# A two-part attention kernel: its output projection on four column tiles, with eight rows a segment projected later

## The chip, the cores and the metric

The kernel runs on one core of one Trainium2 chip. The metric is the device time of one execution in microseconds. A core has five engines that run side by side and wait for each other by semaphores: PE (matrix multiplication), DVE and ACT (vector and scalar work; they copy results out of PSUM), POOL, and SP, which here only issues transfers. Sixteen DMA engines carry the transfers.

## The reference

Part A is a local attention over 2048 rows (32 heads of 20, a window of 8 rows, two apart). The change does not touch it. Part B is an attention with a recurrent memory: 64 segments of 32 rows, each behind 8 memory rows that are the previous segment's output.

```python
M, seg = 8, 32                      # Dm = 640, H = 32 heads of Dh = 192, L = M + seg = 40
mem = mem0
for s in range(64):
    h = concatenate([mem, x[:, 32 * s:32 * s + 32]], axis=1)       # 40 rows
    q, k, v = h @ Wq, h @ Wk, h @ Wv                               # 640 -> 32 x 192 each
    p = softmax(where(mask, q @ k.T * scale, -1e9))                # a row sees the memory and rows up to its own
    o = (p @ v) @ Wo                                               # 32 x 192 -> 640
    mem = o[:, :M]                                                 # the next segment's memory
    outs.append(o[:, M:])
```

The first 8 of the 40 output rows are needed at once, for the next segment. The other 32 are only output.

## The kernel before, in words

Part A comes first. Part B is then a loop of 64 calls of `segment(s)`, and nearly the whole time is spent there. The order of the PE instructions is the order of the program text (a manual schedule); the other engines' instructions are placed by a scheduler.

*Rows.* The 40 rows of a segment are kept as 32 "main" rows (8 memory rows and the first 24 rows of x) and 8 "late" rows (the last 8 of x). A pass over the main rows is `project32` (line 443): 32 rows fill 32 columns of the array, so four matmuls with 384 columns of the weights each run on four column tiles at once. The late rows of four segments are projected together, 32 at a time, ahead of their use, which is what `ahead`, `turn_late` and the tables `STREAMED` and `RENEW` are about; each segment renews one k group and one v group in this way, and the q group of the next segment.

*Groups.* The 32 heads are worked on in four groups of 8. For each group: `project_qk` (q and k, turned by `turn` so that heads lie on partitions), `scores` (line 515), `softmax`, `put_p`, `turn_p` (line 547), `values`, `mix` (line 564; the copies of its four results into the tile `OT` are line 423's, on ACT and DVE in turn), and `project_out(Y, g)` (line 578). OT holds, for each of the group's 12 chunks of 128 rows of (head, element), 40 columns: 32 main rows and 8 late rows. The groups are interleaved by hand in `segment`, so that PE has other work while a softmax or a copy is under way.

*Output projection.* The 24 weight units `o` hold two chunks each. For each chunk two matmuls of 64 columns of OT (40 rows and 24 columns that are not used) and 320 columns of the weights run on two column tiles, one for each half of the 640 outputs, and all 48 chunks are summed in the PSUM tile `Y`. At the end of the segment one ACT copy moves Y into `row` (line 643), `memory_rows` (line 589) turns the first 8 rows and puts them into the next segment's input `HX`, and two transfers on POOL's queue write 32 rows of output (line 650). The last matmuls of the look-ahead q projection stand between project_out(Y, 3) and memory_rows.

*Weights.* Some of the weight units stay in SBUF, and 23 of them do not: 13 of q, k and v with 384 KB and 10 of `o` with 320 KB. They are copied once into DRAM (`wcopy_...`) and loaded again in every segment, through a ring of five slots named `t`: `get_unit` (line 394) issues the load on SP's queue, in the order of use. The load into a slot waits until the matmuls of the unit that used it five places before have ended. SP's queue also loads the next segment's rows, once a segment.

The functions that the change touches:

## Time and profile before

| | |
|---|---|
| median of 3 runs | 2027.26 us (2017.42 to 2029.16) |
| the profiled execution | 2024.66 us, of it 2022.8 us span |
| PE busy | 1945.4 us, 96% of the span |
| DVE, ACT, POOL busy | 1128.3, 725.6, 193.6 us |
| queue of SP's transfers | 87.9% of the 16 DMA engines' time |
| all transfers | 596.29 MB, 295 GB/s in the mean |
| granted PE clock | 0.994 of full speed |

The profile is of one execution. Its groups of instructions give the busy time, the number and the mean length of each kind, and the idle time ahead of them with what ended it; its chain of waits follows the work that ended last, back from the end, each step to what released it. Matmuls are pipelined: several are under way at once, and a matmul's length is not its share of PE's time; that is read from how far apart blocks of them start. A segment takes 28 to 29 us.

### The profile page before, as it was taken

To read this page: it belongs to the slowest core of one execution; us is meant where nothing else is said; L and a number is where in the kernel's file an instruction comes from. 1 tells how busy PE (TensorE), PEld (TensorE's weight loads), DVE (VectorE), ACT (ScalarE), POOL (GpSimd) and SP (SyncE) were. 2 spreads that over 40 slices of the span, in tenths; PEclk is the share of its full clock that TensorE was granted. 3 is DMA by queue.
4 is the path that set the end of the run, shared out by engine and by line. 5 is a ranking of instruction groups with operands and counts; after the bars stand their busy time and mean duration, and the time that the engine had idled before them with its cause. 6 is when DMAs were issued, how large, how long until landed. Compare 5 with 4: busy or idle time off the path is not lost.

```text
span 2022.8 us, 97144 instructions
## 1 busy us (share of the span) xinstructions
PE 1945.4 (96%) x42512; PEld 1243.6 (61%) x42512; DVE 1128.3 (56%) x3622; ACT 725.6 (36%) x2126; POOL 193.6 (10%) x674
## 2 busy tenths in 40 slices
PE   7989999999999999999999999999999999999998
PEld 4656666666666666666666666666666665666665
DVE  5875555555555455555555555555555554555554
ACT  3543333333333333333333333333333333333333
POOL 2000000110001101001001001101001001110110
PEclk9999999999999999999999999999999999999999
DMA  9927999999899999999999989999899988989997
GB/s 343 311 76 269 311 300 305 301 302 307 290 305 304 299 288 312 302 304 303 303 299 297 308 292 311 305 303 299 296 298 303 298 304 284 303 293 300 305 302 257
DMA packets 270123, 596.29 MB, mean 295 GB/s; under 512 B 61065, under 2 KB 72841, under 8 KB 269385
## 3 DMA queue, kind: packets, MB, share of 16 engines
q1 hardware_dynamic: 264770, 585.97, 87.9%
q8 instruction: 333, 5.46, 1.1%
q0 software_dynamic: 4928, 4.11, 0.6%
q14 instruction: 92, 0.75, 0.1%
HBM read 576.85 MB, written 18.87 MB: 295 GB/s over the span
## 4 chain that ended last, share of the span: by engine, by line
PE 71%; DMA 19%; DVE 6%; ACT 1%; issue 1%; SPq 1%; POOL 0%; DVEq 0%; POOLq 0%; ACTq 0%
PE acc L443 33%; PE Y L578 18%; DMA t<-wcopy_k 8%; DMA t<-wcopy_o 6%; PE pt L456 6%; PE Sps L515 4%; PE OTps L564 4%; PE pq L95 2%; PE pt L547 2%; DVE sb L423 2%; DMA out_dram<-row 2%; DMA t<-wcopy_v 1%; PE po L161 1%; DMA wcopy_o<-in_B_Wo_dram 1%; PE py L172 1%
## 5 line engine op out<-in xcount | busy, mean ns | idle before, releaser
L443 PEld LDWEIGHTS <-HX 128*32 128x32 bf16 x19380 | 462.7, 96 | 274.3 <-issue 46.5
L578 PEld LDWEIGHTS <-OT 128*64 128x64 bf16 x6144 | 316.8, 109 | 131.0 <-ACT OT L423 20.0
L578 PE MATMUL Y<-wres_o,OT 128*64 128x320 bf16 x3584 | 344.3, 302 | 2.2
L443 PE MATMUL acc<-wres_q,HX 128*32 128x384 bf16 x6460 | 332.6, 328 | 0.5 <-ACT sb L423 0.2
L443 PE MATMUL acc<-t,HX 128*32 128x384 bf16 x4200 | 309.1, 328 | 12.9 <-DMA t<-wcopy_k 10.1
L578 PE MATMUL Y<-t,OT 128*64 128x320 bf16 x2560 | 277.7, 303 | 10.0 <-DMA t<-wcopy_o 9.2
L423 DVE CAST sb<-acc 128x384 bf16<-128x384 f32 x322 | 178.8, 556 | 186.6 <-PE acc L443 171.3
L443 PE MATMUL acc<-wres_v,HX 128*32 128x384 bf16 x4844 | 276.5, 328 | 0.1
L528 ACT ACTIVATE t<-t 128x160 f32<-128x160 f32 x256 | 86.1, 336 | 439.4 <-DVE t L527 439.4
L443 PE MATMUL acc<-wres_k,HX 128*32 128x384 bf16 x3876 | 224.8, 327 | 0.3 <-issue 0.3
L522 DVE SCALAR_TENSOR_TENSOR t<-Sps,mask 128x160 f32<-128x160 f32 x256 | 82.8, 323 | 214.6 <-PE Sps L515 186.6
L423 ACT CAST sb<-acc 128x384 bf16<-128x384 f32 x324 | 153.6, 474 | 125.1 <-PE acc L443 123.5
L456 PE MATMUL pt<-ident,sb 128*128 128x128 bf16 x1938 | 179.4, 221 | 6.9 <-DVE sb L423 1.7
L423 DVE CAST OT<-OTps 128x120 bf16<-128x120 f32 x512 | 125.5, 271 | 97.4 <-PE OTps L564 96.8
L488 POOL COPY QT<-Lb 128x96 bf16<-128x96 bf16 x252 | 67.4, 267 | 1112.0 <-PE Sps L515 955.2
L456 PEld LDWEIGHTS <-sb 128*128 128x128 bf16 x1938 | 110.2, 97 | 82.3 <-issue 32.3
L515 PEld LDWEIGHTS <-QT 128*64 128x64 bf16 (+1 forms) x4096 | 118.9, 109 | 55.1 <-issue 40.5
L423 ACT CAST OT<-OTps 128x120 bf16<-128x120 f32 x512 | 106.0, 258 | 110.7 <-PE OTps L564 110.4
L515 PE MATMUL Sps<-KT,QT 128*64 128x40 bf16 (+1 forms) x4096 | 137.0, 188 | 2.2 <-DVE KT L423 1.0
L530 DVE TENSOR_REDUCE sm<-t 128x4 f32<-128x160 f32 x256 | 81.8, 320 | 78.7 <-ACT t L528 78.7
L564 PEld LDWEIGHTS <-Vst 32*128 32x128 bf16 (+1 forms) x4096 | 62.2, 97 | 82.3 <-issue 60.5
L564 PE MATMUL OTps<-PT,Vst 32*128 32x40 bf16 (+1 forms) x4096 | 109.7, 192 | 0.0
(75 smaller groups left out, 1916.0 us busy)
## 6 DMA issues: line engine op xcount, KB each, us to landing
t<-wcopy_o SPq DMA_DIRECT2D x640, 320.0 KB, 4.3
t<-wcopy_k SPq DMA_DIRECT2D x512, 384.0 KB, 4.8
t<-wcopy_v SPq DMA_DIRECT2D x320, 384.0 KB, 4.8
wres_q<-in_B_Wq_dram SPq DMA_DIRECT2D x20, 384.0 KB, 7.7
wres_v<-in_B_Wv_dram SPq DMA_DIRECT2D x15, 384.0 KB, 7.8
wres_k<-in_B_Wk_dram SPq DMA_DIRECT2D x12, 384.0 KB, 7.7
wres_o<-in_B_Wo_dram SPq DMA_DIRECT2D x14, 320.0 KB, 6.7
wcopy_o<-in_B_Wo_dram SPq DMA_DIRECT2D x10, 320.0 KB, 8.1
```

The source lines that it names most:

```text
L95: nc.tensor.matmul(pq[32 * d:32 * d + 32], lhsT=wcol[:, k, t, 4 * c + d, :], rhs=xTs[s][:, k, :], start=(k == 0), stop=(k == 4), tile_posi ...
L423: (nc.scalar.copy if copies["n"] % 2 else nc.vector.tensor_copy)(dst, src)
L443: nc.tensor.matmul(ps[n][32 * j:32 * j + 32, :], lhsT=X[:, dc, :], rhs=w[:, 384 * j:384 * j + 384], start=(dc == 0), stop=(dc == 4), tile_ ...
L456: nc.tensor.matmul(pt[:, c], lhsT=sb[:, 128 * c:128 * c + 128], rhs=ident, start=True, stop=True)
L488: nc.gpsimd.tensor_copy(tokens(T)[:, :, 32:L], b[:])
L515: nc.tensor.matmul(Sps[64 * g2:64 * g2 + 64, a, :], lhsT=QT[lo:hi, L * cc:L * cc + 64], rhs=KTt[lo:hi, cc, :], start=(g2 not in seen), sto ...
L522: nc.vector.scalar_tensor_tensor(out=t1[:], in0=Sps[:], scalar=scale, in1=mask[:].unsqueeze(1).to_broadcast([128, 4, L]), op0=ALU.mult, op ...
L528: nc.scalar.activation(t1[:], t1[:], ACTF.Exp)
L530: nc.vector.tensor_reduce(out=sm[:], in_=t1[:], axis=AX.X, op=ALU.add)
L547: nc.tensor.transpose(pt[:, late, :], P[:, late].rearrange("p a n -> p (a n)"), ident)
L564: nc.tensor.matmul(dst, lhsT=V[32 * a:32 * a + 32, e0:e1], rhs=PT[32 * a:32 * a + 32, late, half, :], start=(wide and late == 0 and half = ...
L578: nc.tensor.matmul(Y[64 * gv:64 * gv + 64, :], lhsT=OT[:, L * c:L * c + 64], rhs=w[:, n:n + 320], start=(i == 0 and r == 0), stop=(i == 23 ...
```

## The change

- `project_out` takes the 32 main rows alone. The two chunks of a unit go to four column tiles of 32: even chunks to rows 0 to 63 of Y (a half of the outputs in each 32), odd chunks to rows 64 to 127. `add_pairs` adds the two, with two ACT copies and two DVE additions, into a buffer of the tag `Vst`.
- The 8 late rows of OT are copied on POOL into a tile `OL` after each `mix`; once a segment OL goes to a DRAM tile `OW`. In the last segment they are loaded back, 16 segments at a time, into the places of resident weights that are no longer used (`joined` makes one tile of those), and `project_late` projects 128 rows at a time behind the last segment, with the whole array.
- Of the five weight chunks of the look-ahead q projection, one instead of three stands before project_out(Y, 3), and four instead of two behind it.
- The tables of streamed units change: 12 of k and v and 11 of `o` are streamed in a segment, 23 as before.

```diff
-STREAMED = {"k": ((0, 4), (0, 4), (0, 3), (0, 3)), "v": ((0, 1), (1,), (2,), (2,)),
-            "o": (0, 4, 6, 8, 11, 14, 17, 18, 22, 23)}
+STREAMED = {"k": ((0, 3), (0, 2, 4), (0, 3), (3,)), "v": ((0, 3), (1,), (1,), ()),
+            "o": (0, 4, 5, 6, 9, 11, 12, 16, 18, 22, 23)}
 SLOT = 1536
 RENEW = {0: ("k0", "v2"), 1: ("k1", "v3"), 2: ("k2", "v0"), 3: ("k3", "v1")}
 BLOCKS = 18
...
         v = t[:, 0:unit_cols(u)]
         return v.rearrange("p (k d) -> p k d", k=2) if u[0] == "o" else v
+    joined = {("q", 0): [], ("q", 1): [], ("q", 2): [], ("v", 1): []}
+
     def place_resident(pool, units):
         for u in units:
-            res[u] = pool.tile([128, unit_cols(u)], BF16, name="wres_%s%d_%d" % u)[:]
+            part = joined.get(u[:2])
+            if part is None:
+                res[u] = pool.tile([128, unit_cols(u)], BF16, name="wres_%s%d_%d" % u)[:]
+                continue
+            if not part:
+                n = sum(v[:2] == u[:2] for v in units)
+                part.append(pool.tile([128, n, 1536], BF16, name="wres_%s%d" % u[:2]))
+            res[u] = part[0][:, sum(v[:2] == u[:2] for v in res), :]
     def load_resident(units, engs):
         for k, u in enumerate(units):
...
     place_resident(respool, resident[:n_pre])
     dpool = ctx.enter_context(tc.tile_pool(name="b_copy", bufs=1, space=bass.MemoryType.DRAM))
     XW = dpool.tile([n_seg, 2 * SEG, Dm], BF16, name="xwindows")
+    OW = dpool.tile([n_seg, 128, 48 * M], BF16, name="olate")
     def copy_windows():
...
     P = cpool.tile([128, 2, 4, 32], BF16, name="P")
-    OT = cpool.tile([128, 12 * L + PADW], BF16, name="OT")
+    OT = cpool.tile([128, 12 * L], BF16, name="OT")
+    OL = cpool.tile([128, M, 48], BF16, name="OL")
     free = [cpool.tile([128, 12, M], BF16, name=f"Lb{i}") for i in range(BLOCKS)]
     late = {}
     LV = [cpool.tile([128, 384], BF16, name=f"Lv{g}") for g in range(GROUPS)]
     nc.gpsimd.memset(P[:], 0.0)
-    for t in [QT, OT]:
-        nc.gpsimd.memset(t[:, t.shape[1] - PADW:], 0.0)
+    nc.gpsimd.memset(QT[:, 12 * L:], 0.0)
     copies = {"n": 0}
...
                                          tile_position=(32 * a, col))
         for a in range(4):
             evacuate(OT[:, 3 * L * a:3 * L * a + 3 * L], ps[a][:].rearrange("p k n -> p (k n)"))
+        nc.gpsimd.tensor_copy(OL[:, :, 12 * g:12 * g + 12].rearrange("p n c -> p c n"), tokens(OT)[:, :, 32:L])
     def project_out(Y, g, pairs=range(6)):
         for a in pairs:
...
             for r in range(2):
                 c = 2 * a + r
                 for gv in range(2):
-                    n = 640 * r + 320 * gv
-                    nc.tensor.matmul(Y[64 * gv:64 * gv + 64, :], lhsT=OT[:, L * c:L * c + 64],
-                                     rhs=w[:, n:n + 320], start=(i == 0 and r == 0), stop=(i == 23 and r == 1),
-                                     tile_position=(0, 64 * gv))
+                    n, at = 640 * r + 320 * gv, 64 * r + 32 * gv
+                    nc.tensor.matmul(Y[at:at + 32, :], lhsT=OT[:, L * c:L * c + 32], rhs=w[:, n:n + 320],
+                                     start=(i == 0), stop=(i == 23), tile_position=(0, at))
+
+    def add_pairs(Y):
+        t1 = one.tile([128, 4, L], FP32, tag="t1")
+        odd = t1[:].rearrange("p a n -> p (a n)")
+        Ysb = one.tile([128, 384], BF16, tag="Vst")
+        for h in range(2):
+            nc.scalar.copy(odd[64 * h:64 * h + 64, :], Y[64:128, 160 * h:160 * h + 160])
+        for h in range(2):
+            nc.vector.tensor_tensor(out=Ysb[0:64, 160 * h:160 * h + 160], in0=Y[0:64, 160 * h:160 * h + 160],
+                                    in1=odd[64 * h:64 * h + 64, :], op=ALU.add)
+        return Ysb
     def memory_rows(s, Ysb):
         pt = ps_x.tile([128, 5, M], FP32, tag="x")
...
                 c0, c1 = max(128 * dc, 320 * gv), min(128 * dc + 128, 320 * gv + 320)
                 if c0 < c1:
                     lo = c0 - 128 * dc
-                    nc.tensor.matmul(pt[lo:lo + c1 - c0, dc, :], lhsT=Ysb[:, c0 - 320 * gv:c1 - 320 * gv],
-                                     rhs=ident[:, 64 * gv:64 * gv + M], start=True, stop=True,
+                    nc.tensor.matmul(pt[lo:lo + c1 - c0, dc, :], lhsT=Ysb[0:64, c0 - 320 * gv:c1 - 320 * gv],
+                                     rhs=ident[0:64, 32 * gv:32 * gv + M], start=True, stop=True,
                                      tile_position=(0, lo))
         nc.vector.tensor_copy(HXs[(s + 1) % 2][:, :, 0:M], pt[:])
+
+    LATE = n_seg // 4
+
+    def late_tokens(b):
+        wide = joined[(("q", 0), ("q", 1), ("q", 2), ("v", 1))[b]][0]
+        return wide[:].rearrange("p n c -> p (n c)")[:, 0:LATE * 48 * M]
+
+    def load_late(b):
+        nc.gpsimd.dma_start(late_tokens(b).rearrange("p (s n) -> p s n", s=LATE), OW[LATE * b:LATE * b + LATE].rearrange("s p n -> p s n"))
+
+    def project_late(b):
+        X = late_tokens(b).rearrange("p (t c) -> p t c", c=48)
+        ps = [ps_acc.tile([128, 384], FP32, tag="acc", name=f"late{gv}") for gv in range(2)]
+        for i in range(24):
+            w = get_unit(("o", i, 0))
+            for r in range(2):
+                c = 2 * i + r
+                for gv in range(2):
+                    n = 640 * r + 320 * gv
+                    nc.tensor.matmul(ps[gv][:, 0:320], lhsT=X[:, :, c], rhs=w[:, n:n + 320],
+                                     start=(c == 0), stop=(c == 47))
+        rows = out2.rearrange("(s n) d -> s n d", n=SEG)[LATE * b:LATE * b + LATE, SEG - M:SEG]
+        for gv in range(2):
+            if gv:
+                y = one.tile([128, 384], BF16, tag="Vst", name="y")[:, 0:320]
+            else:
+                y = one.tile([128, 4, L], FP32, tag="t1", name="y")[:].rearrange("p a n -> p (a n)").bitcast(BF16)
+            evacuate(y, ps[gv][:, 0:320])
+            nc.gpsimd.dma_start(rows[:, :, Dm + 320 * gv:Dm + 320 * gv + 320], y)
     def segment(s):
         last = s + 1 == n_seg
...
         project_out(Y, 1, range(4, 6))
         mix(2, PT[2], V[2])
         V[3] = values(s, 3)
+        if last:
+            load_late(0)
+            load_late(1)
+            load_late(2)
         project_out(Y, 2, range(0, 4))
         PT[3] = turn_p()
         project_out(Y, 2, range(4, 6))
         mix(3, PT[3], V[3])
+        nc.gpsimd.dma_start(OW[s], OL[:].rearrange("p n c -> p (n c)"))
+        if last:
+            load_late(3)
+        else:
+            gl = (s + 1) % 4
+            ql = project32([ahead(s + 1)], "q", gl, range(0, 1))
+        project_out(Y, 3)
+        Ysb = add_pairs(Y)
         if not last:
-            gl = (s + 1) % 4
-            ql = project32([ahead(s + 1)], "q", gl, range(0, 3))
-        project_out(Y, 3)
-        row = one.tile([128, 4, L], FP32, tag="t1")
-        Ysb = row[:].rearrange("p a n -> p (a n)").bitcast(BF16)
-        nc.scalar.copy(Ysb, Y[:])
-        if not last:
-            project32([ahead(s + 1)], "q", gl, range(3, 5), ql)
+            project32([ahead(s + 1)], "q", gl, range(1, 5), ql)
             sb = to_sb(ql[0])
             memory_rows(s, Ysb)
             turn_late(sb, "q", gl, s, s + 1)
         for gv in range(2):
-            nc.gpsimd.dma_start(out2[SEG * s:SEG * s + SEG, Dm + 320 * gv:Dm + 320 * gv + 320],
-                                Ysb[64 * gv + M:64 * gv + L, :])
+            nc.gpsimd.dma_start(out2[SEG * s:SEG * s + SEG - M, Dm + 320 * gv:Dm + 320 * gv + 320],
+                                Ysb[32 * gv + M:32 * gv + 32, 0:320])
     load_x(0)
     load_resident(early, [nc.sync])
     with tc.manual_schedule(engines={mybir.EngineType.PE}):
         for s in range(n_seg):
             segment(s)
+        for b in range(4):
+            project_late(b)
 def run_all(ctx, tc, A_x, A_wqkv, A_wo, B_x, B_mem0, B_Wq, B_Wk, B_Wv, B_Wo, out, ident):
```

## The prediction

> **What bounds the kernel now.** I read the head of the page first, then the chain of waits in one segment of part B, then the groups of instructions, and last the transfers. The page:

> ```profile
> PE 1945.4 (96%) x42512; PEld 1243.6 (61%) x42512; DVE 1128.3 (56%) x3622; ACT 725.6 (36%) x2126; POOL 193.6 (10%) x674
> q1 hardware_dynamic: 264770, 585.97, 87.9%
> t<-wcopy_o SPq DMA_DIRECT2D x640, 320.0 KB, 4.3
> t<-wcopy_k SPq DMA_DIRECT2D x512, 384.0 KB, 4.8
> ```

> PE is busy 96% of the span, but the 16 DMA engines are busy 88% as well, nearly all with weights that part B streams anew in every segment: 23 units through five slots `t`. A unit takes 4.3 us (320 KB) or 4.8 us (384 KB) from issue to landing. Who waits, on PE:

> ```profile
> PE acc L443 <- DMA t<-wcopy_k: 10.1, 32, 0.9
> PE Y L578 <- DMA t<-wcopy_o: 9.2, 23, 0.8
> PE pt L547 <- DVE P L540: 6.1, 23, 0.7
> ```

> So PE sets the pace, and waits for units only 10.1 + 9.2 us, with 1.1 us for v: 0.3 us in each of 64 segments. The chain shows one stretch of a segment and how near the transfers are (start, length, what):

> ```profile
> 1024.44 0.93 PE acc L443 x20
> 1025.36 0.39 PE OTps L564 x32
> 1025.76 0.93 PE acc L443 x20
> 1026.68 0.27 PE pt L456 x3
> ...
> 1026.96 0.33 PE pt L547 x2
> 1027.29 1.79 PE Y L578 x24
> ...
> 1030.57 4.79 DMA t<-wcopy_o
> 1035.36 0.04 issue
> 1035.40 0.46 PE Y L578 x4
> ...
> 1036.26 1.74 PE acc L443 x40
> 1038.00 1.21 PE Y L578 x16
> ...
> 1041.08 1.75 PE Y L578 x24
> ```

> Forty matmuls of line 443 take 1.74 us and twenty 0.93 us, so one of 384 columns on four column tiles costs 0.81 / 20 = 40.5 ns. Twenty-four of project_out (line 578, 320 columns on two column tiles) take 1.75 us and sixteen 1.21 us: 67.5 ns each. The chain runs through a 4.79 us transfer although PE hardly idles: ring and PE are both nearly critical. The span is 2022.8 us, the profiled execution 2024.66 us; sums are made against the latter, 2.6 us below the median of the runs (2027.26).

> **What the change removes.** project_out goes from two tiles of 64 columns to four of 32, with the same 96 matmuls a segment. The nearest row is line 443, the same shape with 384 columns: 40.5 x 320/384 = 33.8 ns. Each saves 33.7 ns, 96 x 33.7 = 3.24 us a segment, 64 segments: **-207 us**. Bounds: nothing (if line 443's rate did not carry over) and -207; I take the whole, since only the column count differs.

> **What it adds at the segment's end.** Two covers get thinner: eight matmuls of the look-ahead q projection move from before project_out(Y, 3) to after it, and one ACT copy of Y becomes add_pairs: two ACT copies, then two DVE adds. The end before (start, length):

> ```profile
> 1040.59 0.42 ACT L423 CAST OT<-OTps 128x120 bf16<-128x120 f32 x2 [0.84 <-PE OTps L564]
> 1041.01 0.46 PE L578 MATMUL Y<-t,OT 128*64 128x320 bf16 x4
> 1042.92 0.43 ACT L643 CAST row<-Y 128x320 bf16<-128x320 f32 x1 [1.90 <-issue]
> 1043.40 0.47 PE L589 MATMUL pt<-ident,row 128*128 128x8 bf16 x6
> 1044.21 1.00 PE L443 MATMUL acc<-wres_q,HX 128*32 128x384 bf16 x20
> ```

> mix(3) starts at 1040.02, so the next segment starts 4.19 us later. After: the first quarter of OT is copied 0.57 us after mix(3)'s start for 0.21 to 0.26 us, so project_out starts at about 0.88 (0.99 before). It lasts 0.81 us, and Y is readable at about 1.98. Then two ACT copies of 64x160 at about 0.29 (128x160 bf16 is 0.29 on ACT; the bounds are 0.24 for 96 columns and 0.34 for line 528's exp), and one DVE add after the last copy at 0.32 (line 522's 128x160 from PSUM). With 0.06 us between engines memory_rows starts at about 3.05. From there to the next segment's first matmul was 0.81 us: 3.86. The end gains 0.33 us where the 24 matmuls alone would give 0.81: 0.48 back, x63 = **+30 us** (15 to 45).

> **What else loses its cover.** turn_p(3) comes a median 0.71 us after its P is ready (0.50 to 1.3), and 24 faster matmuls lie between scores(3) and it, 0.81 us less: about 0.15 us of new wait. The QT and KT copies of scores(3) had 0.58 us to spare and lose 0.54; mix(3)'s PT copy had 0.31 and loses 0.27: 0.05 together. 0.2 x 64 = **+13 us** (5 to 30).

> **Off the path.** POOL gets four copies to OL a segment, at 0.27 us each by line 488's 128x96 rows, and one more issue (0.5 us by line 650): 1.6 us in 26 on an engine that is 10% busy. In its order each OL copy stands right after its mix, and the next mix's copies into OT, which wait for it, come over 2 us later. Behind it on POOL stand the late-token copies for QT and KT that scores waits for; with 1 us spare there I cost it at nothing. If that cover went, each stalled mix would cost 0.3 us, 77 us in all. The issue of OW[s] stands ahead of the two output issues and of the next QT copy, which scores(0) wants only some 6 us later. The output's tile is now a `Vst` buffer, whose next writer is values(0), later than `t1`'s.

> **The late rows.** Four batches of 24 units x 4 = 384 matmuls of the full array. The nearest row is part A's output line 172, 128x320, which starts one every 136 ns: 52 us. In the five-slot ring, 11 streamed units a batch and some pairs with 3.7 us between them (need below) give about 1.3 us a batch, 5 us; three hand-overs of a PSUM tile to its evacuation 2 us. The last copy and output issue resemble today's tail. **+59 us** (54 to 72). load_late issues 2048 short rows four times on POOL; the nearest rows are 0.50 us for 32 and 0.55 us for 128 rows, which gives 1.6 us, or 8 us by a proportion: once, **+3 us** (0 to 25), while 6.3 MB more cross the DMA engines.

> **The ring, the largest unknown.** Bytes a segment stay (8192 KB before, 8128 KB and 96 KB of OL after), as do the 23 units, but the segment gets shorter. A slot is free when its unit's last matmul ends; the unit five places on is then issued. I call lead the PE work from that last matmul's start to that fifth unit's first. It must cover the matmul's own 0.30 us (302 ns is the mean of one in the group of line 578), about 0.1 us of issue and semaphores at both ends, and the landing: 4.7 us for o, 5.2 for k and v. Before, the same adding gives no lead under 4.5 us and a handful at 4.5 to 5.0, in keeping with 0.3 us of waits. After, one at a time:
> - o5 follows the slot of k2's chunk 0: 0.74 + 0.39 + 0.93 + 0.27 + 0.33 from the chain above and 20 matmuls of project_out at 33.8 ns, 0.68: 3.3 us. In the two kinds of segment (of four) that also renew k2 or v1, 4.1. Short by 1.4 or 0.6, mean 1.0.
> - o23 follows o11: about 4.1 us, 4.9 where v3 is renewed. Mean 0.4.
> - k2's chunk 0 has 4.4 us in half of the segments: mean 0.4. v0's 4.7 in half: 0.25. o0 and o4: 0.1.
> These make 2.1 us a segment. A wait lengthens the leads that hold it, so not all add up; 1.3 to 2.1, and I take 1.6, which is 1.3 more than now: **+83 us** (20 if landings get shorter, 200 if the fuller ring lengthens them).

> Sum: -207 + 30 + 13 + 59 + 3 + 83 = -19; 2024.66 - 19 = 2006, and I say **2005 us**. Of a gain of 207 us nine tenths are spent again.

> **Rivals.**
> *The ring keeps up.* The landings above are those of a loaded queue. A 10 KB SP transfer lands in 2.3 us by the page and 384 KB at the 403 GB/s of the window from 1015 to 1020 us takes 0.98: 3.3 us on an empty queue. Against it: the queues are 88% busy and medians are 4.3 and 4.8. If needs fell to about 4 us, only o5 would wait, some 0.2 us, and the time would be 2024.66 - 207 + 30 + 13 + 55 + 3 - 8 = 1911; halfway, 1955. [...]

> *The ring takes over: slower.* PE no longer idles the queue, so four or five units are always under way, and landings go to 5.2 us for o and 5.7 for k and v (in the chain around 1012 us one took 6.11 us). Each lead short now is short by another 0.9, and o0, o4, o18 and o22 join: about 3.5 us a segment, 3.2 more than now, +205: 2127. The middle, 2.4 more: 2075. It decides from 1.6 us of added waits a segment; 0.1 us of landing is worth some 25 us. The 385 to 400 GB/s of single windows against the 300 of the mean speak against it.

> *The array doesn't run four tiles of 320 columns as it does of 384.* Then nothing is saved and 100 us are added: 2130. Line 443 speaks against it.

> **How the numbers follow.** The forecast, 1980 to 2035, 0.50; the ring keeps up 0.22; the ring takes over 0.24; four tiles gain nothing 0.04. Faster by over 1% (what a measurement of this kernel can tell; below about 2004) is the second and half of the first: 0.46. Within 1%: most of the rest of the first and a little of the third, 0.28. Slower: 0.26. The range, 1945 to 2075, leaves out the far ends of the two ring cases.

> **What would show it.** Per-segment matmul time of project_out near 3.3 us; PE waits for `t<-wcopy_o` and `t<-wcopy_k` of 60 to 130 us in all, most of them at o5 and o23; waits for add_pairs before memory_rows of about 0.5 us a segment; segments of about 27 us; 55 to 65 us behind the last segment. It is wrong if landings move by over 0.2 us either way, if OT's copies wait for POOL, or if project_out's matmuls do not halve.

## The result, and the profile after

The changed kernel takes **2138.97 us** (median of 4 runs, 2124.48 to 2144.14), the kernel before, on the same chip, 2028.21 us (4 runs, 2017.42 to 2034.18). The ratio is 1.0541, with a 95% interval of 1.0473 to 1.0609: slower by 5.4%, where 2005 us was forecast. The profiled execution took 2138.64 us, of it 2136.9 us span, 114 us more than the one before. The granted PE clock was 0.970 of full speed (0.994 before).

The page of the changed kernel (engines: busy time, share, instructions; the queue of SP's transfers: packets, MB, share of the 16 DMA engines' time; the shares of the chain; ring units: number, size, median us from issue to landing):

```profile
PE 1897.7 (89%) x42896; PEld 1156.5 (54%) x42896; DVE 1187.4 (56%) x3754; ACT 741.1 (35%) x2194; POOL 412.5 (19%) x1005
q1 hardware_dynamic: 271106, 596.20, 83.7%
PE 48%; DMA 41%; issue 5%; DVE 4%; ACT 1%; SPq 1%; POOL 0%; POOLq 0%; ACTq 0%; DVEq 0%
t<-wcopy_o SPq DMA_DIRECT2D x748, 320.0 KB, 4.5
t<-wcopy_k SPq DMA_DIRECT2D x512, 384.0 KB, 5.1
```

PE is busy for 48 us less, and the span is longer: PE waits. The chain that ended last runs through transfers for 41% of the span, where it had been 19% (and PE 71%). Landings moved by only 0.2 and 0.3 us. The waits of the changed kernel (what waited, for what: us in all, times, longest):

```profile
PE Y L589 <- DMA t<-wcopy_o: 69.7, 100, 2.5
PE acc L453 <- DMA t<-wcopy_k: 56.5, 103, 2.8
PE pt L610 <- DVE Ysb L599: 34.9, 122, 0.4
PE Y L589 <- DVE OT L433: 6.6, 30, 0.5
PE acc L453 <- DMA t<-wcopy_v: 5.5, 8, 2.2
PE Y L589 <- ACT OT L433: 4.9, 29, 0.2
```

Waits for ring units are 131.7 us against 20.4 before. New are the waits of memory_rows (line 610) for add_pairs (line 599): about two in each segment. How the chain passes through one segment (start, length, what):

```profile
1006.47 0.89 PE Y L589 x20
...
1007.79 7.16 DMA t<-wcopy_k
1014.94 0.04 issue
1014.99 0.35 PE acc L453 x4
1015.33 0.48 PE Sps L525 x16
...
1019.26 4.82 DMA t<-wcopy_o
1024.08 0.04 issue
1024.12 0.32 PE Y L589 x4
```

Twenty matmuls of project_out take 0.89 us at 1006.47, so the array does run four tiles of 320 columns as fast as hoped. But two transfers, 7.16 and 4.82 us, fill 12 of the 17 us that follow: PE has other work during most of them, but it reaches the unit before the transfer has landed, and from there the transfer sets the time. The groups (out<-in, shapes, number | busy us, mean ns | idle before, what ended most of it):

```profile
L589 PE MATMUL Y<-t,OT 128*32 128x320 bf16 x2816 | 218.9, 307 | 84.6 <-DMA t<-wcopy_o 69.7
L589 PE MATMUL Y<-wres_o,OT 128*32 128x320 bf16 x3328 | 184.7, 302 | 1.2 <-issue 1.2
...
L579 POOL COPY OL<-OT 128x96 bf16<-128x96 bf16 x256 | 173.4, 677 | 657.7 <-DVE OT L433 388.6
...
L498 POOL COPY QT<-Lb 128x96 bf16<-128x96 bf16 x252 | 67.5, 268 | 744.4 <-PE Sps L525 676.2
```

PE idles for 1.2 us ahead of the project_out matmuls with resident weights and for 84.6 us ahead of those with streamed ones. The copies to OL take 677 ns where the other 128x96 copy takes 268.

**Where the 114 us are.** I split each profiled execution into part A with segment 0, the next 62 segments (from one segment's first memory_rows matmul to the next's), and the rest. Before: 216.7, 62 x 28.60, 32.8. After: 217.4, 62 x 29.17, and 111.2, which is 42.8 for the last segment and 68.4 for the late rows and the tail. So the loop lost 35 us instead of gaining 78, and the end cost 78 us instead of 59.

### The profile page after: what moved, and what is told of

It is laid out like the page before. It is cut to its first block, busy times and chain, and to the rows that moved or that the text cites. A ratio compares the mean times of both kernels' runs of the same rounds, so it can differ in the third digit from the quotient of the medians.

```text
span 2136.9 us, 98886 instructions
## 1 busy us (share of the span) xinstructions
PE 1897.7 (89%) x42896; PEld 1156.5 (54%) x42896; DVE 1187.4 (56%) x3754; ACT 741.1 (35%) x2194; POOL 412.5 (19%) x1005
## 4 chain that ended last, share of the span: by engine, by line
PE 48%; DMA 41%; issue 5%; DVE 4%; ACT 1%; SPq 1%; POOL 0%; POOLq 0%; ACTq 0%; DVEq 0%
PE acc L453 24%; DMA t<-wcopy_o 21%; DMA t<-wcopy_k 16%; PE Y L589 7%; PE Sps L525 5%; PE pt L466 4%; PE OTps L574 2%; PE pq L95 2%; DMA t<-wcopy_v 2%; PE pt L557 1%; DMA wcopy_o<-in_B_Wo_dram 1%; PE po L161 1%; DMA xwindows<-in_B_x_dram 1%; SPq L366 1%; DVE prod L151 0%
## 5 line engine op out<-in xcount | busy, mean ns | idle before, releaser
L453 PEld LDWEIGHTS <-HX 128*32 128x32 bf16 x19380 | 490.9, 98 | 350.7 <-issue 121.7
L453 PE MATMUL acc<-t,HX 128*32 128x384 bf16 x3876 | 300.8, 336 | 63.7 <-DMA t<-wcopy_k 56.5
L453 PE MATMUL acc<-wres_q,HX 128*32 128x384 bf16 x6460 | 348.1, 339 | 1.0 <-ACT sb L433 0.3
L579 POOL COPY OL<-OT 128x96 bf16<-128x96 bf16 x256 | 173.4, 677 | 657.7 <-DVE OT L433 388.6
L453 PE MATMUL acc<-wres_v,HX 128*32 128x384 bf16 x5168 | 296.8, 334 | 1.4 <-issue 1.4
L589 PE MATMUL Y<-t,OT 128*32 128x320 bf16 x2816 | 218.9, 307 | 84.6 <-DMA t<-wcopy_o 69.7
L453 PE MATMUL acc<-wres_k,HX 128*32 128x384 bf16 x3876 | 254.3, 335 | 0.3 <-ACT sb L433 0.3
L589 PEld LDWEIGHTS <-OT 128*32 128x32 bf16 x6144 | 146.2, 96 | 187.7 <-issue 103.6
L498 POOL COPY QT<-Lb 128x96 bf16<-128x96 bf16 x252 | 67.5, 268 | 744.4 <-PE Sps L525 676.2
L589 PE MATMUL Y<-wres_o,OT 128*32 128x320 bf16 x3328 | 184.7, 302 | 1.2 <-issue 1.2
L525 PEld LDWEIGHTS <-QT 128*64 128x64 bf16 (+1 forms) x4096 | 108.7, 110 | 72.8 <-issue 51.7
## 6 DMA issues: line engine op xcount, KB each, us to landing
t<-wcopy_k SPq DMA_DIRECT2D x512, 384.0 KB, 5.1
t<-wcopy_v SPq DMA_DIRECT2D x256, 384.0 KB, 4.9
wres_q<-in_B_Wq_dram SPq DMA_DIRECT2D x20, 384.0 KB, 7.7
wres_v<-in_B_Wv_dram SPq DMA_DIRECT2D x16, 384.0 KB, 7.7
wres_k<-in_B_Wk_dram SPq DMA_DIRECT2D x12, 384.0 KB, 7.3
```

Of the source, the lines that this page charges most:

```text
L453: nc.tensor.matmul(ps[n][32 * j:32 * j + 32, :], lhsT=X[:, dc, :], rhs=w[:, 384 * j:384 * j + 384], start=(dc == 0), stop=(dc == 4), tile_ ...
L498: nc.gpsimd.tensor_copy(tokens(T)[:, :, 32:L], b[:])
L525: nc.tensor.matmul(Sps[64 * g2:64 * g2 + 64, a, :], lhsT=QT[lo:hi, L * cc:L * cc + 64], rhs=KTt[lo:hi, cc, :], start=(g2 not in seen), sto ...
L579: nc.gpsimd.tensor_copy(OL[:, :, 12 * g:12 * g + 12].rearrange("p n c -> p c n"), tokens(OT)[:, :, 32:L])
L589: nc.tensor.matmul(Y[at:at + 32, :], lhsT=OT[:, L * c:L * c + 32], rhs=w[:, n:n + 320], start=(i == 0), stop=(i == 23), tile_position=(0, at))
```

## The experiments

Times are medians; "a segment" is the mean of the 62. Unless it says otherwise an edit is one to the changed kernel.

**Without the ring, changed kernel and kernel before.** Streamed units are read from resident ones instead (o from o1, k and v from q3's chunk of the same number), so no weights are loaded in the loop and the outputs are not the reference's.

```diff
             return res[u]
+        return get_unit(("o", 1, 0) if u[0] == "o" else ("q", 3, u[2]))
         t = wstream.tile([128, SLOT], BF16, tag="ws")
```

> Leaves out: the changed kernel with every streamed weight unit replaced by one that stays in SBUF, so the five-slot ring carries nothing (wrong weights, the same matmuls). Theory 1 (ring): the changed kernel's segments lose about 2.4 us each to waits for units and its last segment and late rows some 25 us more, so this comes to 1950 to 1975 us, segments of 26.0 to 26.5 us. Theory 2 (clock): PE at half clock in 31 windows of 3.4 to 10 us is what costs; then little is won here, over 2050 us, and the granted clock falls further, because PE is denser. Theory 3 (POOL's copies to OL, 0.68 us each, hold OT): over 2050 us as well, with the clock as now.

> The same done to the kernel before: all streamed units replaced by resident ones. Theory 1: it loses only its 0.3 us of waits a segment, 2028 - 20 = about 2005 us; the gap to the changed kernel without its ring is then what the change is worth on PE alone, about -40 us (-207 for project_out, +160 for the rest). Theory 2: the two without a ring differ by less than that, or the changed one is slower, by its clock.

Measured: the changed kernel 1899.98 us, ratio 0.9369 (0.9345 to 0.9394); the kernel before 1978.66 us, 0.9757 (0.9731 to 0.9782). The page of the changed kernel without a ring:

```profile
PE 1804.4 (95%) x42896; PEld 1124.8 (59%) x42896; DVE 1183.4 (62%) x3754; ACT 737.5 (39%) x2194; POOL 413.3 (22%) x1005
q1 hardware_dynamic: 52802, 49.01, 8.4%
```

On PE alone the change is worth -79 us: segments of 25.76 against 27.83 us (-2.07), and 86.3 us behind the loop against 32.5 (+54). The granted clock is 0.996 without the ring, where theory 2 had it fall further. The ring costs the kernel before 49 us and the changed kernel **239 us**, 0.77 and 3.41 us a segment. That settles which side the loss is on. Both times lie below what the ring theory gave (1950 to 1975 and about 2005 us): the ring costs more than the waits for units that it counted. The rest asks what the 239 us are made of.

**x set to zero** (the rows of part B are copied from a DRAM tile of zeros), because the clock had fallen from 0.994 to 0.970.

> The changed kernel with part B's input rows all zero (the windows are copied from a block of zeros), every instruction and transfer as it is. [...] Theory 2: the half-clock windows of part B vanish (granted clock over 0.99) and the time falls by 30 to 45 us, to about 2100. Theory 1: the clock may recover, but PE then waits for units instead; 2120 to 2139 us.

Measured: 2143.6 us, ratio 1.058 (1.0532 to 1.0629), clock 0.968. The clock is hardly another with zeros (0.968, against 0.970 in the changed kernel), and theory 2, which expected over 0.99, is out: that the data set the clock was my assumption, and no run shows it.

**Without the late rows** (no copy to OL, no OW, no load_late, no project_late; the last 8 output rows of each segment are missing).

```diff
-        nc.gpsimd.tensor_copy(OL[:, :, 12 * g:12 * g + 12].rearrange("p n c -> p c n"), tokens(OT)[:, :, 32:L])
...
-        nc.gpsimd.dma_start(OW[s], OL[:].rearrange("p n c -> p (n c)"))
...
-        for b in range(4):
-            project_late(b)
```

> The changed kernel without the late rows: no copies to OL, no transfer of OL, nothing loaded back, no late projection (eight output rows a segment are not written). Theory 1: the segments stay at 29.2 us and only the end goes, about 78 us: 2055 to 2065 us. Theory 3: the segments get shorter as well, by 0.4 us or more each, and the time is below 2035 us.

Measured: 2051.2 us, ratio 1.013 (1.0084 to 1.0176). A segment takes 28.91 us, 0.26 less (theory 3 asked for 0.4): that is all that POOL's long copies and OL's transfers can cost in the loop. The end falls from 111.2 to 33.4 us.

**Where the next segment's rows are loaded.** In both kernels SP's waits for that load had looked suspicious: 76 us in the kernel before, 146 in the changed one, with ring loads queued behind.

```diff
-        load_x(s + 1)
         tq, tk, V, PT = {}, {}, {}, {}
...
         V[0] = values(s, 0)
+        load_x(s + 1)
```

> The changed kernel with load_x(s + 1), the load of the next segment's rows, placed behind values(s, 0) instead of at the head of the segment; it needs its buffer only at the segment's end. So far it stands in SP's queue ahead of the weight loads for the segment's first k units and waits there for PE (146 us in all, 76 before the change), while slots come free behind it. Theory 1a (the queue is held up at the segment's head): the waits at k1's chunks 2 and 4, about 1.0 us a segment, go; segments 28.0 to 28.3 us, 2060 to 2085 us. Theory 1b (the DMA engines' load alone sets the landings): the same waits turn up elsewhere, 2125 to 2145 us.

> The kernel before with the same later place of load_x. Theory 1a: its ring costs 49 us by the run without a ring, of which the units at the head of the segment hold about a third: 2005 to 2020 us. Theory 1b: 2020 to 2032 us.

Measured: 2141.11 us, 1.0549 (1.0498 to 1.0601), and for the kernel before 2027.17 us, 1.0007 (0.9987 to 1.0027). That theory fell: nothing moves.

**The old table of streamed units, and the old cover** (three chunks of the look-ahead q ahead of project_out(Y, 3)).

```diff
-            ql = project32([ahead(s + 1)], "q", gl, range(0, 1))
+            ql = project32([ahead(s + 1)], "q", gl, range(0, 3))
...
-            project32([ahead(s + 1)], "q", gl, range(1, 5), ql)
+            project32([ahead(s + 1)], "q", gl, range(3, 5), ql)
```

> The changed kernel with the table of streamed units of the kernel before (13 of k and v, 10 of o): as many units, 64 KB more a segment, other places. Theory 1c (places: a unit waits where the PE work between its slot's release and its use is short): the waits at o5 (0.8 us a segment) and k1 go, those at o23 stay, and some new ones come at the v0 pair; 2075 to 2110 us. Theory 1b: the load is the same, so 2130 to 2150 us.

> The changed kernel with the look-ahead q projection split as before the change: three chunks before project_out(Y, 3) and two behind it. My price for the new split was 0.2 us a segment at OT's copies against 0.32 at add_pairs. The lead of o23 grows by 0.3 us here and the wait for add_pairs by 0.3: 2130 to 2145 us, no change. If the end of the segment were what costs, it would move by over 20 us.

Measured: the old table 2113.93 us, 1.0442 (1.0388 to 1.0496); the old cover 2150.69 us, 1.0598 (1.0543 to 1.0652). The old table, between the bands of its two theories, takes the waits from 1.98 to 1.73 us a segment and moves them (o23 alone has then 0.69 us). It is 25 us below the changed kernel, though the intervals of the two ratios overlap: the change's new table was no gain. The old cover is a little above its band: the change's own cover is no loss.

**Eight slots and half the bytes.** Room for three more slots comes from using one chunk of q3's weights in the place of three others. Half bytes: each load brings the first half of a unit's columns and the matmuls read them twice. In both the matmuls and their number stay as they were, and the outputs are not the reference's.

```diff
-    part_b(..., pre=110000, nbuf=5,
+    part_b(..., pre=110000, nbuf=8,
...
```

```diff
-        nc.sync.dma_start(t[:, 0:unit_cols(u)], copied[u])
+        nc.sync.dma_start(t[:, 0:half], copied[u][:, 0:half])
...
```

> The changed kernel with eight slots in the ring instead of five, the same 23 units streamed a segment. The room comes from three resident units of q, which are replaced by a fourth (three chunks of q have wrong weights). Theory 1d (the lead of five slots against a landing of 4.5 to 5 us is the limit): a unit's lead grows from 5.6 to 9 us, nearly all waits go and with them the half-clock windows; 1905 to 1940 us. Theory 1e (what the DMA engines can carry is the limit, at the 300 GB/s that they show before and after): nothing moves, 2110 to 2140 us.

> The changed kernel with five slots and 23 transfers a segment, each of half the columns, which the matmuls read twice (wrong weights). Theory 1d: a landing has a part that does not shrink with the bytes (over 2 us), so it falls to some 3.3 to 3.8 us and the waits shrink to those of o5: 1910 to 1960 us. Theory 1e: half the load, so no waits at all, 1900 to 1905 us. The median landing is the number to read: near 2.4 us if it is all transfer time, over 3 us if most of it is fixed.

Measured: eight slots 1999.6 us, 0.9836 (0.9804 to 0.9869); half the bytes 1917.56 us, 0.9439 (0.9413 to 0.9465). With half the bytes a segment takes 25.81 us, as without a ring, and the landings are (size, median us):

```profile
t<-wcopy_o SPq DMA_DIRECT2D x748, 160.0 KB, 2.6
t<-wcopy_k SPq DMA_DIRECT2D x512, 192.0 KB, 3.3
t<-wcopy_v SPq DMA_DIRECT2D x256, 192.0 KB, 3.0
```

Halving the bytes takes 1.9, 1.8 and 1.9 us off landings of 4.5, 5.1 and 4.9 us. By estimate, as twice that, 3.6 to 3.8 us of a landing go with the bytes and the load that they make, which leaves 0.7 to 1.5 us for a fixed time. The run with eight slots lies between its two bands: PE has hardly a wait for a unit left in the 62 segments, but segments of 27.11 us are still 1.35 above those without a ring. The waits of that run, and the queue that its page calls instruction:

```profile
PE pt L614 <- DVE Ysb L603: 30.4, 106, 0.4
PE OTps L578 <- issue: 23.8, 27, 3.2
PE acc L457 <- issue: 23.2, 25, 2.5
...
PE Y L593 <- issue: 12.0, 16, 3.0
...
q8 instruction: 336, 5.51, 1.1%
```

"issue" means that nothing in the profile released PE. In the loop such gaps come to 60 us in this run and to 10 us with five slots; without a ring and with half the bytes there is hardly one (none and 0.3 us). The trace shows where they stand: PE's 86,043 records of the changed kernel's whole run come to 256 for each of the 336 packets of 16 KB of queue q8 (as many packets as here), and all 49 gaps of over 0.4 us stand at the same place in such a block of 256 (record 193 to 195) and end 1.2 to 1.7 us after the end of a packet. The packets take no longer than without a ring (median 0.97 and 1.01 us), but they come later: in the median one ends 1.7 us before PE reaches that place, against 3.6 us without a ring and 2.9 us with five slots. That PE lacked its own instructions there is my reading of these places, for no view names a packet as what ended a gap; what holds the packets up stays open too.

**Six and seven slots with all the weights**, each further slot paid for by one more streamed unit a segment: k3's chunk 0 for the sixth (below), v3's chunk 2 as well for the seventh.

```diff
-STREAMED = {"k": ((0, 3), (0, 2, 4), (0, 3), (3,)), "v": ((0, 3), (1,), (1,), ()),
+STREAMED = {"k": ((0, 3), (0, 2, 4), (0, 3), (0, 3)), "v": ((0, 3), (1,), (1,), ()),
```

> The changed kernel with six slots, paid for by streaming one more unit of k (k3's chunk 0), 24 a segment; the computation is whole. Theory 1d: the mean lead is 25.8 x 6/24 = 6.4 us instead of 5.6; the ring's cost of 3.4 us a segment falls to 1.0 to 2.0, 1990 to 2060 us. Theory 1e: 4% more bytes, 2140 to 2200 us.

> Seven slots, paid for by one more unit of k and one of v (v3's chunk 2), 25 a segment; the computation is whole. Theory 1d: mean lead 7.2 us; 1950 to 2030 us, under the kernel before if the load of 9 MB a segment, 350 GB/s at 25.8 us, can be carried. Theory 1e: 2200 us and over.

Measured: 2065.21 us, 1.0166 (1.014 to 1.0193), and 2055.08 us, 1.0113 (1.0073 to 1.0152). Both are above the bands of the first theory (1990 to 2060 and 1950 to 2030 us). Waits fall to 0.96 and 0.14 us a segment, but the gaps without a releaser are 46 and 84 us in the loop, and those of over 0.4 us (47 and 76) stand at the same place of the block of 256. The slots give back 74 and 84 of the 239 us.

**Six slots with other units streamed**, and **the kernel before with six and with eight slots.** The table of the first was sought with the PE order of the run without a ring and a simple model of landings. The kernel before with six slots streams v3's chunk 4 as well; with eight it uses one chunk of q3's weights for four, as above.

```diff
-STREAMED = {"k": ((0, 3), (0, 2, 4), (0, 3), (0, 3)), "v": ((0, 3), (1,), (1,), ()),
-            "o": (0, 4, 5, 6, 9, 11, 12, 16, 18, 22, 23)}
+STREAMED = {"k": ((0, 3, 4), (2, 3, 4), (0, 1), (1, 2)), "v": ((4,), (4,), (0,), ()),
+            "o": (0, 1, 6, 8, 9, 12, 13, 16, 21, 22, 23)}
```

> The changed kernel with six slots and 24 streamed units as in the earlier run with six slots (2065), but with other units streamed: the places were sought with the PE order of the run without a ring and a model in which landings grow with the number of transfers under way. Theory A, part of the cost is where the streamed units lie (k1's chunks and the o units at the segment's end stand too close together): waits fall from 0.96 to 0.4 to 0.5 us a segment and the time to 2025 to 2045. Rival B, only bytes and slots count: 2058 to 2072.

> The kernel before with six ring slots instead of five, paid for by one more streamed unit a segment (v3's chunk 4, so 24 units). Theory A, the slots and the load share the cost: without the ring the kernel before took 1979, so its ring costs 49 us, of which 0.35 us a segment (22 us) are waits that the profile names; six slots take nearly all of these away, the 24th unit fills the queue a little more, and the time is 2005 to 2020. Rival B, a fuller queue costs as much as the slot saves (as with the change, where seven slots paid by two units gained only 10 us over six): 2022 to 2035, with PE gaps that no releaser ends.

> The kernel before with eight slots and its 23 units; the room is made by using one chunk of the last head group's q weights in the place of three others, so the output's numbers are not the reference's. With the change, eight slots took all named waits away and still left 1.35 us a segment over the run without a ring, with PE gaps of 61 us in all that nothing in the profile releases. Theory A, these gaps come from a queue that always has seven or eight transfers under way: they appear here too, and the time is 2000 to 2015, 20 to 35 us above the run without a ring (1979). Rival B, they come from the change's own instructions or its faster pace: none here, and 1979 to 1990.

Measured: the new table 2132.57 us, 1.0526 (1.0475 to 1.0577), outside what either theory expected: places matter a great deal (67 us between two tables of 24 units and six slots), and my model of them was wrong. It put three k0 and three k1 units behind each other at the segment's start, and there k0's chunk 4 and k1's chunk 4 now wait 0.59 and 0.41 us a segment. The kernel before with six slots: 2039.07 us, 1.0048 (1.0027 to 1.0068), 4 us above even the rival's band. Its waits fall only from 0.35 to 0.28 us a segment, k's landings grow from 4.8 to 5.4 us, and part A with segment 0 takes 4.6 us longer: the 24th unit costs more than the slot brings, as the rival had it, though without the gaps. With eight slots: 2009.2 us, 0.9903 (0.987 to 0.9936), in the band of the first theory, yet without the gaps that it rested on; the waits for "issue" behind part A come to a few us:

```profile
PE acc L447 <- issue: 2.9, 5, 1.4
...
PE Sps L519 <- issue: 1.3, 3, 0.7
```

So a full queue alone doesn't make these gaps: in the loop eight slots come with 60 us of them in the changed kernel and with 2.7 us here, and no run parts its pace from its own instructions. Here the instruction packets end in the median 2.9 us before their place is reached. And a stream whose units no one waits for still costs the kernel before 30 us. No version that uses all the weights was faster than the kernel before.

## Why the prediction was wrong

By its own steps, for the 62 segments (us a segment; working in the prediction):

| step | predicted | measured |
|---|---|---|
| project_out on four tiles | -3.24 | -3.03 |
| the segment's end | +0.48 | +0.83 |
| turn_p(3) and other lost cover | +0.20 | +0.13 |
| sum on PE, without a ring | -2.56 | -2.07 |
| the ring | +1.3 | +2.64 |
| sum | -1.26 | +0.57 |

The first four rows compare the two runs without a ring block by block; the fifth is 3.41 - 0.77. The table's misses are 0.49 and 1.34 us, times 62: 30 and 83 us. Behind the loop it was 78 us instead of 59. That is the miss of 134 us, to 2 us.

**project_out** was right: within a block one matmul starts every 34 ns, where it was 68 ns. A segment's 96 take 4.03 us to the start of what follows them, 7.06 before; most of what is missing from 3.24 us are 0.19 us of waits for OT's copies, 0.04 before. The rival that four tiles gain nothing is out.

**The segment's end** was mis-sized. The waits for add_pairs are 34.9 us, 0.55 a segment, as named. But memory_rows begins when the first of add_pairs' two additions is done and then waits for the second, and from its first matmul to the next block it takes 0.76 us, not 0.53. I had priced one wait and let memory_rows keep its length.

**The late rows**: the end without a ring is 54 us more than before, as forecast (59, of it 5 for waits on the ring). With the ring it is 78. Fifteen of the 25 us between are the last segment, 42.8 us and without a ring 28.0, because load_late was priced at 3 us. Its four issues take 1.2 us each on POOL, which is cheap; what seems to cost is its 6 MB beside the ring, for in the run without the late rows, which has the ring and no load_late, PE ends 27.4 us behind the loop. The other 10 are the late projection, 63.9 us and without a ring 53.8, which also waits 6.4 us for streamed units. Windows of the last segment (PE, PEld, DVE, ACT, POOL busy; granted clock; DMA share; GB/s) stand here behind three windows around one wait in the loop:

```profile
1086.40:1089.70 3.30, 0.81 (x25) 0.42 (x19) 0.13 (x1) 0.18 (x1) 0.18 (x1) 1.00 0.79 289
1089.80:1093.21 3.41, 3.41 (x80) 1.82 (x78) 2.27 (x9) 0.95 (x4) 1.25 (x3) 0.50 0.64 202
1093.21:1096.62 3.41, 3.24 (x98) 1.74 (x90) 0.71 (x3) 1.08 (x5) 1.04 (x3) 1.00 0.49 159
...
2025.00:2040.00 15.00, 10.36 (x198) 5.94 (x191) 7.08 (x21) 4.56 (x12) 5.68 (x10) 0.96 1.00 345
2040.00:2060.00 20.00, 12.58 (x221) 6.35 (x224) 4.67 (x17) 2.50 (x7) 0.94 (x2) 0.61 0.86 297
```

**POOL's copies** were priced by a row of the same shape, 0.27 us, and take 0.68: that row writes eight elements in a run, these lie 96 bytes apart. (Its reads differ as well, runs of eight instead of one piece, and no run parts the two.) It cost little: without all late-row work the loop gains 0.26 us a segment.

**The ring is the step that failed**, in three ways.

*Where the waits are.* Their sum was not far off: 1.63 us a segment more than before, where 1.3 was taken. But o5 waits 0.54 (1.0 expected), o23 0.34 (0.4), k2's chunk 0 and v0 almost nothing (0.65): their leads, taken from the run without a ring, are 0.1 to 0.7 us longer than the prediction's. In their place stand k1's chunks 0, 2 and 4 with 0.65. They have some of the longest leads there, 6.1 to 6.4 us, so I gave them nothing. But they are issued close together when o18, o22 and o23 end, with the streamed k0 units still under way, and their median landings are 5.7, 6.3 and 6.8 us. I compared every lead with one median landing; a landing was longer with more others under way: for the k units of the loop the median is 3.3, 4.2, 5.1 and 5.5 us with one, two, three and four other units under way at the issue. OL's transfer at the segment's end, which I had priced at its issue alone, seems to add to it: without the late rows these three land in 5.4, 5.8 and 6.3 us and wait 0.42. The median of all units hardly moved (+0.2), and the rule that "it is wrong if landings move by over 0.2 us" looked at the wrong number.

*What a wait costs behind itself.* In the first window above PE waits; the timeline of that stretch:

```profile
1086.19 0.45 PE L589 MATMUL Y<-wres_o,OT 128*32 128x320 bf16 x8
1089.13 0.32 PE L589 MATMUL Y<-t,OT 128*32 128x320 bf16 x4 [2.48 <-DMA t<-wcopy_o]
...
1091.00 1.79 PE L453 MATMUL acc<-wres_v,HX 128*32 128x384 bf16 x20
```

PE idles for 2.48 us, and 0.7 us after it starts again the clock is at 0.50 for 3.41 us: twenty matmuls of line 453 take 1.79 us, and the prediction's chain had 0.93. In the 62 segments the clock is at half for 85 us, 3.4 before, which can cost up to half of that, 0.66 us a segment more. In the loop, runs without these waits have none of it (no ring, half the bytes), and with x at zero it is 99 us; so in these runs it comes with the waits, whatever the data. The stretches of half clock start on a grid of 3.41 us: of the changed kernel's 529 grid windows at full clock behind 200 us, 27 are followed by a window at half, and in these PE was busy for 16 to 65%; only 7 others are as low. I priced a wait at its own length.

*What it adds up to.* The changed kernel runs the same matmuls in the same order with and without a ring, so the steps from one matmul's start to the next's can be compared one by one. Of 3.41 us a segment, 2.60 stand at the matmuls that wait for a unit: 1.98 are the waits as the profile counts them, and the rest comes because a wait counts from the end of the matmul ahead, about 0.3 us after its start, while without a wait the next would have started long before that end (34 ns after that start within a block of project_out). Matmuls at half clock have 0.55, the gaps without a releaser 0.24, and all others 0.02. The same for the kernel before gives 0.54 of its 0.77 at waiting matmuls, and with eight slots 0.30 of its 0.47 at waits for DVE and ACT; what lengthens those beside the stream stays open.

**The rivals.** "The ring takes over" came closest: it gave 2127 at 3.2 us of added ring time, and 2.64 with a dearer end made 2139. Its mechanism, landings of 5.2 and 5.7 everywhere, was seen only for the units that are issued together, and o0, o4, o18 and o22, which it named, wait 0.1 us in all. "The ring keeps up" is out. By its own estimate (2.3 us and 384 KB at the 403 GB/s of one window, 0.98 us) halving the bytes would take 0.5 us off a k or v unit's landing; the run took 1.8 to 1.9 off. No run here shows a unit's transfer by itself.

## What to carry to other kernels

Where one engine's work and a stream of weights are both near the bound, price a faster engine on the kernel without the stream and with half its bytes first: here these two runs showed that 79 us were to be had on PE and that the stream would take them. Compare each lead with the landing at that place, with all that is under way (k units here: 3.3 us with one other unit, 5.5 us with four), not with the median. A PE wait cost more here than the profile's gap (2.60 us a segment against 1.98), by what the matmuls ahead would have overlapped, and half-clock time came with the waits (85 us in the 62 segments, 3.4 before). And slots that take the waits for units away can bring other gaps: with eight, nearly all those waits went, and PE had 60 us of gaps that nothing in the profile ends.
